# A gated mix of a spectral layer and a SwiGLU on one core: comparisons placed in the second product stage, another VectorE order in the last stage, 4 KB rows of output, a branch hint

## The chip, the core and the metric

The kernel runs on one core of one Trainium2 chip. Its engines are TensorE (PE, whose weight loads the profile lists as PEld), VectorE (DVE), ScalarE (ACT), GpSimd (POOL) and SyncE (SP, which here only issues DMAs). The metric is the time of one execution on the device, in microseconds; the figure of a version is the median of its runs.

## The reference

With x of 2048 x 512, D = 512 and F = 1376, all in float32:

```python
a = einsum("bsd,ed->bse", x, dft_hid_re)
b = einsum("bsd,ed->bse", x, dft_hid_im)
y = einsum("ts,bse->bte", dft_seq_re, a) - einsum("ts,bse->bte", dft_seq_im, b)
h = silu(x @ w1) * (x @ w3)          # 2048 x 1376
g = sigmoid((x * gate_w).sum(-1, keepdims=True))
out = g * y + (1 - g) * (h @ w2)
```

The four DFT matrices are inputs. They are made of cosines and sines, whose rows and columns repeat with signs; the kernel uses that, but only after it has compared the entries it was given with one another.

## The kernel before

Each float32 product is made of three products in a faster format: an operand is split into a high part (rounded by ACT, `high`, L115) and a low part (the rest, taken by DVE, `low`, L118), and `mm3` (L129) adds high x high, high x low and low x high in one bank of accumulators. `split` is `high` and then `low`. So each operand of PE costs one instruction of ACT and one of DVE, about 1.1 us each for 128 x 1024 values.

The work goes in three stages.

**Gate and up products.** F is cut in 11 chunks of 128 columns, the last with 96; rows of x go in two groups. An item is a chunk and a group, with the products of a fast 2 x 2 scheme. `store_h(n, k, h)` (called from L309 on, on POOL's DMA queue) puts the finished h of an item in memory, in `hs`.

**Products with w2.** 22 steps (`HSTEPS`): 11 chunks for one half of the rows, then 11 for the other. A step is 24 products of 128 x 512 into eight banks `H0` to `H7`. Within step m, ACT and DVE make high and low part of the h of step m+2 (`high_h`, `low_h`, the tiles `ht`, read into `hr`), SP starts to load the h of step m+4 (`load_h`), and w2's parts follow the same way. The last chunk, with 96 rows, is done apart: `load_stacked` reads 64 of its rows and two copies of the other 32 into one tile and four pieces of those 32 into a second, and `stacked` multiplies them so that no product has an operand of 32 rows alone, except eight small ones. At the end of each half, ACT writes (1 - g) h w2 as tiles `nb` of two blocks of 128 rows (L1266); those of the first half go to memory (`nbsp`) and come back later (`load_nb`), those of the second half stay in four buffers of their own, `NBK`.

In the gaps of this stage stands everything that the Fourier part needs. A hand-written planner sets it: a `task` has an engine, a cost in us, a load and a number of 4 KB-wide buffers (list `F4`, taken with `wide`, given back with `free`). `load_ahead(t)` starts loads for tasks in order, as long as buffers are left beyond the reserve `RES` and the paced time `NEXT` allows; `work(engine, t, us)` puts tasks whose load was started at least `LAND` us before into the program, up to `us`. In the loop of the steps, `credit` is the time DVE may spend on tasks: 3.0 us a step in the first half, 3.75 in the second. The tasks are:

- the comparisons: 60 tiles of 128 x 1024 entries of the matrices for sequences (`compare_one` and `compare_two`, `equal`, L555), each against the first tile of its group (`rep`), and some smaller ones. The groups are O1a, O1b, O2 and E2. `accum_out` counts the equal entries in columns of `tail`. The late tiles of E2 (i of 8 and more) are compared as two halves of 128 x 2 x 256 with signs +1 and -1.
- the folding of x: sums and differences of rows that meet the same factors (`make_pair`, `odd_part`, `even_part`, tiles `xm`, `xf`), with `fix_a` and `fix_b`, which put two lone rows in their places.
- `mov`, the parts of the matrix for sequences, and `dt`, those of the matrix for the hidden dimension.
- `lone`, which POOL does once, right ahead of step 0: sums and differences of the four quarters of one row of 1024 and of a few other edge values (L973 to L997).

**The last stage.** PE makes folded sums O1 (two halves), O2 and E2 (two halves) from x and the matrix for sequences, each in a pair of banks (`next_two`, four pairs in turn). For O1, ACT copies one part (`e`, L1336), DVE adds and subtracts the other (`s`, L1337 and L1338), and all are split into `z_O`, `z_E`. DVE puts one late comparison behind the `s` of each half of O1, and `work("D", end + 14.0, 2.5)` puts comparisons ahead of the low part of the second z_E. `verdict` (L565 and L566) then counts the columns of `tail` that hold what they should. After that come ten output units: 12 products each with `dt` (Y), g times the result plus `nb` (`r`, L1391, for two blocks of rows or one; the last unit in two pieces, L1395), and a DMA of `r` to `out` on SP (L1399, L1397), with rows of 2 KB. Behind unit 1, `verdict_end` sums the count over partitions by one small product (`count`, L569, in a pair of banks of its own) and DVE turns it into a flag. Behind unit 4's sums PE, ACT and POOL read the flag, and at the end `tc.If(bad > 0)` (L1412) runs the general way, without any folding, where an entry had not been as expected.

```python
    work_until(end + 16.0, range(n_late))
    verdict()
    ...
        if u == 1:
            verdict_end(next_two("count"))
```

Of the kernel before, what the change touches and what calls it, by code (L numbers as in the profile page):

```python
# [13 lines left out]
P = 128  # L14
S = 2048
D = 512
# [15 lines left out]
def fnet_swiglu_gate_kernel(  # L32
# [106 lines left out]
    NZ = misc.shape[-1] - 32 - 2 * (NS + 8)  # L139
    gs = dram.tile([NTB, 1, 512], F32, tag="gs", name="gs")  # L140
    nbsp = dram.tile([S // P, P, D], F32, tag="nbsp", name="nbsp")
    hs = dram.tile([NC, P, S], F32, tag="hs", name="hs")
    wbsp = dram.tile([NC, P, 2, 4, 256], F32, tag="wbsp", name="wbsp")
# [160 lines left out]

    def store_h(n, k, h):

        c, g = ITEMS[n]
        b = 2 * g + k
        nc.gpsimd.dma_start(hs[c][:, b * TB : (b + 1) * TB], h)  # L309
# [285 lines left out]
    def load_ahead(t):  # L595
        CLOCK[0] = t
        load_pairs(t)
        for i in ORDER[:LIMIT[0]]:
            _, _, _, _, f, need, temps = QUEUE[i]
            if i in LOADED:  # L600
                continue
# [148 lines left out]
    def compare(kind):  # L750
# [4 lines left out]
        LAST[kind] = [task("D", 1.24 if kind == "E2" and i > 7 else 1.16, lambda i=i: compare_one(kind, i), (),  # L755
# [45 lines left out]
    def compare_small():  # L801
        d = task("D", 0.4, differ_small, (), lambda: load_t(72, misc[:, 32:]), 1)
        task("A", 0.7, add_small, (d,))
# [43 lines left out]
    def fix_a():  # L847

        nc.gpsimd.tensor_copy(at_first(XR["O1a"], 1), row_v)
        nc.gpsimd.memset(at_first(XR["w", 0], 1), 0.0)  # L850

    def fix_b():
        w = at_first(XR["w", 1], 0)
        nc.gpsimd.tensor_add(edge[:1, :128], w[:, :128], w[:, 128:])
        nc.gpsimd.tensor_sub(edge[:1, 128:256], w[:, :128], w[:, 128:])
        nc.gpsimd.tensor_copy(w, row_u)
# [105 lines left out]
    def lone():  # L962
# [3 lines left out]
        ROWS.extend(wide(f"row{k}") for k in range(2))  # L966
        r0, r1 = ROWS
        nc.sync.dma_start(r0[:1], edges[:, :1024])
        nc.sync.dma_start(rowm[:1], edges[:, 1024:])
        nc.sync.dma_start(spc, misc[:, :32])  # L970
        a, b = r0[:1, :512], r0[:1, 512:]
        u, v = r1[:1, :512], r1[:1, 512:]
        g.tensor_add(u, a, b)  # L973
        g.tensor_sub(v, a, b)
        g.tensor_add(u[:, :256], u[:, :256], u[:, 256:])
        g.tensor_sub(v[:, :256], v[:, :256], v[:, 256:])
# [5 lines left out]
        s = spc.rearrange("p (w t) -> p w t", w=2)  # L982
# [26 lines left out]
        return u[:, :256], v[:, :256]  # L1009
# [61 lines left out]
    R, LEFT = F - (NC - 1) * P, {}  # L1071
    assert R == 96

    def load_stacked(m, half):
# [3 lines left out]
        h = hs[NC - 1][:, half * 1024 : (half + 1) * 1024]  # L1078
        for to, lo, hi in ((0, 32, 96), (64, 0, 32), (96, 0, 32)):
            nc.sync.dma_start(a[to : to + hi - lo], h[lo:hi])  # L1080
        v = h[:32].rearrange("p (a g n) -> p a g n", a=2, g=4)
        for g in range(4):
            nc.sync.dma_start(b[32 * g : 32 * g + 32, :256].rearrange("p (a n) -> p a n", a=2), v[:, :, g])
# [81 lines left out]
    def stacked(to, j, h, w):  # L1165
# [5 lines left out]
        for k in range(8):  # L1171
            p, at = slice(32 * (k % 4), 32 * (k % 4) + 32), 512 + k // 4 * P
# [25 lines left out]
    F4.extend((f4d, f"f4_{k}") for k in range(20, 24))  # L1198
    NBK = [(f4d, f"f4_{k}") for k in range(24, 28)]
# [8 lines left out]
    spc = edge[:, :32]  # L1208
# [11 lines left out]
    for m, (half, c) in enumerate(HSTEPS):  # L1220
        again = m >= NC
        i = m % NC
        last = i == NC - 1
        if m == NC:
            GAP[0], RES[0] = 1.6, 1
        if i == 0:
            H = [bank(b, f"H{half}_{j}") for j, b in enumerate(HB)]
        h, w = HT[m][1], WT[i]
        for j in range(8):
# [19 lines left out]
            if j == 3:  # L1249
                credit += 5.0 if m + 2 >= len(HSTEPS) else 3.75 if again else 3.0  # L1250
# [9 lines left out]
            if last:  # L1260
                k = 8 * half + j
                if j % 2 == 0:
                    nbt = take(NBK if again else F4, [P, 1024], F32, f"nb{k}")
# [3 lines left out]
                if j % 2 and not again:  # L1267
                    nc.gpsimd.dma_start(nbsp[k - 1 : k + 1].rearrange("k p n -> p k n"),
                                        nbt.rearrange("p (k n) -> p k n", k=2))
                    free(NB.pop(k // 2))  # L1270
# [44 lines left out]

    UNITS = [("O1", 512 * v + P * a, 512 * v + 256 + P * a, 2, 0) for a in range(2) for v in range(2)]
# [4 lines left out]
    def load_nb(u):  # L1321
        NB[u] = wide(f"nbr{u}")
        nc.sync.dma_start(NB[u].rearrange("p (k n) -> p k n", k=2),
                          nbsp[2 * u : 2 * u + 2].rearrange("k p n -> p k n"))
# [4 lines left out]
    Z, O1 = {}, {}  # L1329
    for p in range(2):  # L1330
        t = O1[p] = next_two(f"O1_{p}")
# [3 lines left out]
        e, s = wide(f"e{p}"), wide(f"s{p}")  # L1335
# [10 lines left out]
    two = next_two("O2")  # L1346
    for p in range(2):
        ps = two[:, 512 * p : 512 * p + 512]
        forms(ps[:, :256], ps[:, 256:], ("O2",), range(2), p)
    t = parts("z_O2").rearrange("p h a n -> p h (a n)")  # L1350
    split(t[:, 0], t[:, 1], two)
    for p in range(2):
        Z["O2", p] = t[:, :, 512 * p : 512 * p + 512]
    for p in range(2):
# [313 lines left out]
```

## Time and profile before

| | |
|---|---|
| median of three runs | 353.34 us (352.95 to 355.42) |
| the profiled execution, its time | 352.38 us |
| the same, its span in the profile | 350.6 us |
| mean clock granted to TensorE | 0.998 of full speed |
| PE, products of the w2 stage (`H`) | 512 of 380 ns |
| DVE, comparisons of whole and half tiles (L555, `t`) | 54, busy 57.0 us |
| POOL, issues of `hs` from `h` | 34 of 543 ns |
| moved by DMA | 102.13 MB, 291 GB/s in the mean |

The time is that of the whole execution; the span goes from the first to the last record of the profile, 1.78 us less. Busy time is that of instructions in execution. The groups of tiles show who paces whom:

```profile
L129 PE MATMUL H<-w2t,ht 128*128 128x512 f32 x512 | 111.3, 380 | 0.0
...
L555 DVE SCALAR_TENSOR_TENSOR t<-t,rep 128x1024 f32<-128x1024 f32 (+1 forms) x54 | 57.0, 1103 | 0.0
L115 ACT ACTIVATE ht<-hr 128x1024 fp32r<-128x1024 f32 (+1 forms) x20 | 21.0, 1058 | 44.8 <-PE H L129 44.7
L309 POOL DMA_DIRECT2D hs<-h x34 | 18.5, 543 | 121.9 <-DVE h L367 98.3
```

A row gives line, engine, operation, what is written from what with its shape, how often, then busy time and the mean of one in ns, and then the engine's idle time ahead of such instructions and what ended most of it. PE had no idle time ahead of the 512 products with w2, whereas ACT sat idle 44.7 us ahead of the high parts of h, until products of PE were done.

### The profile page before, as it was taken

The page shows a single profiled execution, that of the slowest core. Times are in us where ns is not written, and L with a number is a line of the kernel's source. Part 1 is how long each engine was busy: PE and PEld are TensorE (multiplying, and loading weights), DVE is VectorE, ACT ScalarE, POOL GpSimd, SP SyncE. Part 2 cuts the span into 40 slices and gives each one's busy share as a digit, 9 for nine tenths or more (in the row PEclk, how much of TensorE's full clock was granted, in tenths as well). Part 3 has the DMA queues.
Part 4 walks back from the last instruction along what each step waited for, and adds up shares of the span by engine and source line. Part 5 has one row for each costly group of instructions (what it writes and reads, how often), then busy time and mean ns, then how long its engine had stood idle before and what let it go on. Part 6 is the DMA issues. An engine that isn't in the chain of part 4 may idle for free.

```text
span 350.6 us, 4984 instructions
## 1 busy us (share of the span) xinstructions
PE 343.7 (98%) x1697; PEld 299.3 (85%) x1697; DVE 312.9 (89%) x499; ACT 173.1 (49%) x264; POOL 61.9 (18%) x124
## 2 busy tenths in 40 slices
PE   8999999999999999999999999999999999999993
PEld 4888888888888888888888888888888888889993
DVE  4999989999889988888887799999997998898993
ACT  5875766656546464334442273134679632306400
POOL 0001212112111111111100009981063001000000
PEclk9999999999999999999999999999999999999999
DMA  7638966979559599999999829997156879999066
GB/s 279 259 146 314 351 226 244 371 269 323 215 159 352 219 380 407 417 388 400 407 397 409 325 81 349 396 314 256 65 179 243 296 239 303 367 416 395 10 237 250
DMA packets 32353, 102.13 MB, mean 291 GB/s; under 512 B 5698, under 2 KB 6722, under 8 KB 30276
## 3 DMA queue, kind: packets, MB, share of 16 engines
q1 hardware_dynamic: 27652, 81.84, 64.1%
q0 software_dynamic: 4672, 19.93, 14.6%
q8 instruction: 15, 0.25, 0.3%
q14 instruction: 14, 0.11, 0.1%
HBM read 77.63 MB, written 24.13 MB: 290 GB/s over the span
## 4 chain that ended last, share of the span: by engine, by line
PE 93%; DVE 3%; DMA 1%; ACT 0%; issue 0%; SPq 0%; DVEq 0%
PE H L129 32%; PE X L129 31%; PE Z L129 16%; PE Y L129 11%; PE C L129 3%; DVE t L555 1%; DMA xs_B<-xt 1%; DVE z_O L118 1%; PE O L129 1%; DVE s L1337 0%; DVE z_E L118 0%; DVE s L1338 0%; PE Y_odd L129 0%; ACT e L1336 0%; DVE r L1395 0%
## 5 line engine op out<-in xcount | busy, mean ns | idle before, releaser
L129 PE MATMUL H<-w2t,ht 128*128 128x512 f32 x512 | 111.3, 380 | 0.0
L129 PEld LDWEIGHTS H<-w2t,ht 128*128 128x128 f32 x512 | 96.5, 189 | 14.4 <-issue 0.7
L129 PE MATMUL X<-xo,wb 128*128 128x512 f32 x378 | 88.6, 379 | 0.0
L129 PEld LDWEIGHTS X<-xo,wb 128*128 128x128 f32 x378 | 71.4, 189 | 10.1
L555 DVE SCALAR_TENSOR_TENSOR t<-t,rep 128x1024 f32<-128x1024 f32 (+1 forms) x54 | 57.0, 1103 | 0.0
L115 ACT ACTIVATE ht<-hr 128x1024 fp32r<-128x1024 f32 (+1 forms) x20 | 21.0, 1058 | 44.8 <-PE H L129 44.7
L309 POOL DMA_DIRECT2D hs<-h x34 | 18.5, 543 | 121.9 <-DVE h L367 98.3
L129 PE MATMUL X<-xo,wa 128*128 128x512 f32 x126 | 30.7, 380 | 0.0
L129 PE MATMUL Y<-xo,wa 128*128 128x512 f32 x126 | 30.6, 379 | 0.0
L129 PE MATMUL Z<-xo,wb 128*128 128x512 f32 x126 | 30.6, 379 | 0.0
L129 PE MATMUL Z<-xo,wa 128*128 128x512 f32 x126 | 30.6, 379 | 0.0
L379 ACT ACTIVATE h<-X 128x512 f32<-128x512 f32 x21 | 12.5, 596 | 34.3 <-PE X L129 32.5
L118 DVE TENSOR_TENSOR ht<-hr,ht 128x1024 fp32r<-128x1024 f32 (+1 forms) x18 | 22.0, 1224 | 5.5 <-ACT ht L115 5.4
L129 PEld LDWEIGHTS X<-xo,wa 128*128 128x128 f32 x126 | 23.7, 189 | 3.6 <-ACT h L379 0.3
L129 PEld LDWEIGHTS Y<-xo,wa 128*128 128x128 f32 x126 | 23.8, 189 | 3.4
L129 PEld LDWEIGHTS Z<-xo,wb 128*128 128x128 f32 x126 | 23.8, 189 | 3.4
L129 PEld LDWEIGHTS Z<-xo,wa 128*128 128x128 f32 x126 | 23.8, 189 | 3.4
L115 ACT ACTIVATE wa<-ws 128x768 fp32r<-128x768 f32 (+2 forms) x21 | 16.9, 806 | 11.8 <-PE Z L129 10.6
L118 DVE TENSOR_TENSOR wa<-ws,wa 128x768 fp32r<-128x768 f32 (+1 forms) x22 | 19.3, 879 | 3.8 <-ACT wa L115 3.6
L358 DVE TENSOR_TENSOR u<-u,X 128x512 f32<-128x512 f32 x21 | 14.4, 686 | 7.7 <-PE X L129 7.6
L383 DVE TENSOR_TENSOR h<-h,u 128x512 f32<-128x512 f32 x21 | 14.5, 688 | 5.7 <-ACT h L379 5.7
L266 ACT ACTIVATE s<-X 128x512 f32<-128x512 f32 x21 | 12.5, 596 | 12.0 <-PE X L129 11.7
(219 smaller groups left out, 461.5 us busy)
## 6 DMA issues: line engine op xcount, KB each, us to landing
t<-wt SPq DMA_DIRECT2D x46, 512.0 KB, 10.1
hs<-h POOLq DMA_DIRECT2D x34, 256.0 KB, 6.3
wbsp<-wb POOLq DMA_DIRECT2D x8, 1024.0 KB, 5.3
wb<-wbsp SPq DMA_DIRECT2D x8, 1024.0 KB, 11.6
hr<-hs SPq DMA_DIRECT2D x16, 512.0 KB, 4.5
tt<-wt SPq DMA_DIRECT2D x7, 1024.0 KB, 6.2
ws<-w SPq DMA_DIRECT2D x11, 512.0 KB, 5.0
xs_B<-xt SPq DMA_DIRECT2D x8, 512.0 KB, 4.4
```

The lines of the kernel that those rows point to most:

```text
L115: nc.scalar.activation(hi, src, AF.Copy)
L118: nc.vector.tensor_sub(lo, src, hi.bitcast(F32))
L129: nc.tensor.matmul(ps.rearrange("p (n a) -> p n a", a=2), u, turns(v)[:, some], **kw)
L266: nc.scalar.activation(s1, x, AF.Copy)
L309: nc.gpsimd.dma_start(hs[c][:, b * TB : (b + 1) * TB], h)
L358: nc.vector.tensor_add(u4, u4, x)
L379: nc.scalar.activation(g1, x, AF.Silu)
L383: nc.vector.tensor_mul(g1, g1, u4)
L555: nc.vector.scalar_tensor_tensor(t, t, sign, r, op0=ALU.mult, op1=ALU.is_equal, accum_out=place(n))
```

## The change

Ten things change in the text; the products, and what is compared, stay.

- **Output.** `out` and `nbsp` are laid out as eight blocks of 128 x 1024, so that an output unit of two blocks is stored in rows of 4 KB; the host puts the rows in order.
- **The late E2 tiles** are laid out on the host so that a whole tile of 1024 is compared at once with a repeated quarter of `rep`.
- **The last chunk.** `store_h` writes its 96 rows, a copy of 32 of them, and the pieces (`rest`): three DMAs in place of one. `load_stacked` reads two tiles in place of seven pieces. The eight small products take other rows.
- **`lone`.** The row of 1024 comes as 128 x 4 + 128 x 4 values spread over partitions; the four sums are of 128 x 4 and 128 x 2, and one DMA to memory (`rowsp`) and one back make a row of it, both on POOL's queue.
- **`fix_a` and `fix_b`.** The two copies go from POOL to ACT, the two edge sums from POOL to DVE.
- **Buffers.** The four of `NBK` join `F4`; the second half's `nb` tiles are taken from `F4` too. The first half's `nb` buffers are given back in step 13. `RES` is 6 from step 8 to 10.
- **The planner.** `credit` is 3.15 and 3.9 us a step in place of 3.0 and 3.75, less 1.25 in the very last one; tasks without a load are taken up only when the tasks they wait for have been issued.
- **The last stage's order.** No comparison stands ahead of the low part of the second z_E; that low part moves behind unit 0's sums, and `verdict` ahead of it.
- **The count.** `verdict_end` comes right behind unit 1's products, ahead of its sums, in unit 1's own pair of banks.
- **The branch.** PE gets a hint, `mark_branch_hint_location`, at unit 7's place in the text, that the branch of `tc.If` is likely to be taken.

The core of the diff:

```diff
+        nc.gpsimd.dma_start(to[:R], h[:R])
+        nc.gpsimd.dma_start(to[R:], h[64:R])
+        nc.gpsimd.dma_start(rest[g, 64 * k : 64 * k + 64].rearrange("(q p) n -> p q n", q=2),
+                            h[64:R].rearrange("p (q n) -> p q n", q=2))
...
-            if i in LOADED:
+            if i in LOADED or not f and any(k not in ISSUED for k in after):
...
-            tv, rv = halves(t), halves(r)
-            for h in range(2):
-                equal(tv[:, :, h], rv[:, :, h], 1.0 - 2.0 * h, 512)
+            q = i % 4
+            rv = r[:, 256 * q : 256 * q + 256][:, None].to_broadcast([P, 4, 256])
+            equal(t.rearrange("p (k n) -> p k n", k=4), rv, 1.0 - 2.0 * (q % 2), 1024)
...
-        a, b = r0[:1, :512], r0[:1, 512:]
-        u, v = r1[:1, :512], r1[:1, 512:]
+        a, b = spc[:, 32:36], spc[:, 36:]
+        u, v = rows[:, :4], rows[:, 4:]
         g.tensor_add(u, a, b)
         g.tensor_sub(v, a, b)
...
+        g.dma_start(rowsp.rearrange("k p n -> p k n"), rows.rearrange("p (k n) -> p k n", k=2)[:, :, :2])
+        row = ROWS[0][:1, :512]
+        g.dma_start(row, rowsp.rearrange("k p n -> (k p n)")[None])
...
-        nc.gpsimd.tensor_copy(at_first(XR["O1a"], 1), row_v)
+        nc.scalar.activation(at_first(XR["O1a"], 1), row_v, AF.Copy)
...
-        for to, lo, hi in ((0, 32, 96), (64, 0, 32), (96, 0, 32)):
-            nc.sync.dma_start(a[to : to + hi - lo], h[lo:hi])
...
+        nc.sync.dma_start(a, hs[NC - 1][:, half * 1024 : (half + 1) * 1024])
+        nc.sync.dma_start(b[:, :256], rest[half])
...
-    F4.extend((f4d, f"f4_{k}") for k in range(20, 24))
-    NBK = [(f4d, f"f4_{k}") for k in range(24, 28)]
+    F4.extend((f4d, f"f4_{k}") for k in range(20, 28))
...
-                credit += 5.0 if m + 2 >= len(HSTEPS) else 3.75 if again else 3.0
+                credit += 5.0 if m + 2 >= len(HSTEPS) else 3.9 if again else 3.15
+                if again and c == NC - 1:
+                    credit -= 1.25
...
-        if p:
-            work("D", end + 14.0, 2.5)
-        split(*(z[:, h].rearrange("p (v n) -> p v n", v=2) for h in range(2)),
-              two.rearrange("p (v n) -> p v n", v=2)[:, :, :258])
-    work_until(end + 16.0, range(n_late))
+    low(*put_e2(0))
+    work_until(end + 14.0, range(n_late))
     verdict()
+    last_e2 = put_e2(1)
...
+        if u == 1:
+            verdict_end(ps)
...
+        if n == 2:
+            nc.sync.dma_start(out[u], r)
+        elif not split_up:
+            nc.sync.dma_start(out_of(k), r[:, :D])
         free(r)
-        if u == 1:
-            verdict_end(next_two("count"))
+        if u == 0:
+            low(*last_e2)
+        if u == 7:
+            tc.mark_branch_hint_location("general", "LikelyTaken", engines=(mybir.EngineType.PE,))
...
-    with tc.If(bad > 0):
+    with tc.If(bad > 0, label="general"):
```

`put_o1`, `put_o2` and `put_e2` hold the text that stood in the loops before; `put_e2` does the products and the high part and returns what `low` needs.

On DVE, from the low part of the second half of O1 to the sums of unit 1 (t are compared tiles, rep what they are compared with, tail the counts, r rows of the output), there stood:

```order
L118 TENSOR_TENSOR z_O_2993<-s_2989,z_O_2993 128x1024
L118 TENSOR_TENSOR z_O_3025<-O_2998,z_O_3025 128x1024
L118 TENSOR_TENSOR z_E_3042<-E_0_3028,z_E_3042 128x516
L555 SCALAR_TENSOR_TENSOR t_2862,tail<-t_2862,rep_1964 128x2x256 x2
L118 TENSOR_TENSOR z_E_3061<-E_1_3045,z_E_3061 128x516
L565 TENSOR_SCALAR tail<-tail 128x1
L566 SCALAR_TENSOR_TENSOR tail<-tail 128x80
L1391 SCALAR_TENSOR_TENSOR r_3104<-Y_3091,tail,nb_2867 128x512 x2
L1391 SCALAR_TENSOR_TENSOR r_3121<-Y_3108,tail,nb_2876 128x512 x2
L570 TENSOR_SCALAR tail<-count 1x1
```

and now:

```order
L118 TENSOR_TENSOR z_O_2990<-s_2958,z_O_2990 128x1024
L118 TENSOR_TENSOR z_O_3020<-O_2993,z_O_3020 128x1024
L118 TENSOR_TENSOR z_E_3037<-E_0_3023,z_E_3037 128x516
L577 TENSOR_SCALAR tail<-tail 128x1
L578 SCALAR_TENSOR_TENSOR tail<-tail 128x80
L1419 SCALAR_TENSOR_TENSOR r_3095<-Y_3082,tail,nb_2869 128x512 x2
L118 TENSOR_TENSOR z_E_3080<-E_1_3064,z_E_3080 128x516
L582 TENSOR_SCALAR tail<-Y_3100 1x1
L1419 SCALAR_TENSOR_TENSOR r_3115<-Y_3100,tail,nb_2878 128x512 x2
```

The two half comparisons have left this stretch, the second z_E stands behind unit 0's two sums, the verdict's two instructions ahead of them, and the flag (L570, now L582) is made ahead of unit 1's sums.

On POOL, at the head of `lone`, ahead of step 0 of the w2 products (row is one row of 1024 values, rows its quarters spread over partitions, few some edge values), there stood:

```order
L973 TENSOR_TENSOR row_1894<-row_1893 1x512
L974 TENSOR_TENSOR row_1894<-row_1893 1x512
L975 TENSOR_TENSOR row_1894<-row_1894 1x256
L976 TENSOR_TENSOR row_1894<-row_1894 1x256
L978 TENSOR_TENSOR few<-rowm 1x2
L979 TENSOR_TENSOR few<-rowm 1x2
```

and now:

```order
L983 TENSOR_TENSOR rows<-edge 128x4
L984 TENSOR_TENSOR rows<-edge 128x4
L985 TENSOR_TENSOR rows<-rows 128x2
L986 TENSOR_TENSOR rows<-rows 128x2
L987 DMA rowsp<-rows 128x2x2
L989 DMA row<-rowsp 1x16x32
L991 TENSOR_TENSOR few<-rowm 1x2
L992 TENSOR_TENSOR few<-rowm 1x2
```

The long sums on one partition have become short ones on all, and two DMAs stand behind them.

On ACT, from the leftover of w2 to the first `nb` tiles at the end of the first half (ht are high parts of h, w2t of w2, xf of folded x), there stood:

```order
L115 ACTIVATE left<-w2r_2166 128x512
L1162 ACT_TABLE_LOAD
L1162 ACTIVATE tail<-tail 128x16
L1163 ACTIVATE tail<-tail 128x16
L115 ACTIVATE ht_2279<-hr_2202 128x1024
L115 ACTIVATE w2t_2281<-w2r_2166 128x512
L115 ACTIVATE ht_2319<-hr_2248 128x1024
L115 ACTIVATE xf_O1a<-xm_O1a 128x1024
L115 ACTIVATE ht_2360<-hr_2290 128x1024
L1266 ACTIVATE nb_2362<-H_0_1929,tail 128x512
```

and now:

```order
L115 ACTIVATE left<-w2r_2187 128x512
L784 ACTIVATE size,tail<-dh_2169 128x516
L861 ACTIVATE xo_O1a<-row 1x256
L1170 ACT_TABLE_LOAD
L1170 ACTIVATE tail<-tail 128x16
L1171 ACTIVATE tail<-tail 128x16
L115 ACTIVATE ht_2316<-hr_2231 128x1024
L115 ACTIVATE w2t_2318<-w2r_2187 128x512
L868 ACTIVATE xw_2194<-row 1x256
L115 ACTIVATE ht_2358<-hr_2281 128x1024
L115 ACTIVATE ht_2396<-hr_2327 128x1024
L1282 ACTIVATE nb_2398<-H_0_1940,tail 128x512
```

The two row copies of `fix_a` and `fix_b` (L861, L868) stand here now, the second ahead of the h of step 11, and the high part of folded x has moved behind the `nb` tiles.

More of the change, by code (lines that the diff above doesn't have):

```diff
@@ L1008, in lone @@
         g.tensor_sub(lb[:, 3], sob[:, 0], sob[:, 1])
-        return u[:, :256], v[:, :256]
+        return row[:, :256], row[:, 256:]
     for kind in ("O2", "O1a", "O1b", "E2"):
@@ L1207, in fnet_swiglu_gate_kernel @@
     edge, rowm, few = (own(k, [P, n]) for k, n in (("edge", 258), ("rowm", 520), ("few", 5)))
-    spc = edge[:, :32]
+    spc = edge[:, :40]
+    rows = own("rows", [P, 8])
     two, lone_a, lone_b = own("two", [P, 2, 2, 8]), own("lone_a", [P, 8]), own("lone_b", [P, 4, 2, 2])
@@ L1262, in fnet_swiglu_gate_kernel @@
                 if j % 2 == 0:
-                    nbt = take(NBK if again else F4, [P, 1024], F32, f"nb{k}")
+                    if again:
+                        F4.insert(0, F4.pop(next(i for i, (p, _) in enumerate(F4) if p in (f4d, f4_a))))
+                    nbt = wide(f"nb{k}")
                     NB[k // 2] = nbt
@@ L1322, in load_nb, with put_o1 @@
         NB[u] = wide(f"nbr{u}")
-        nc.sync.dma_start(NB[u].rearrange("p (k n) -> p k n", k=2),
-                          nbsp[2 * u : 2 * u + 2].rearrange("k p n -> p k n"))
+        nc.sync.dma_start(NB[u], nbsp[u])
     for u in range(4, 8):
         load_nb(u)
-    Z, O1 = {}, {}
-    for p in range(2):
-        t = O1[p] = next_two(f"O1_{p}")
+    Z = {}
+    def put_o1(p):
+        t = next_two(f"O1_{p}")
+        e, s = wide(f"e{p}"), wide(f"s{p}")
         for par in range(2):
@@ L1345, in fnet_swiglu_gate_kernel, with put_o2, put_e2 @@
         Z["O1", p] = z
[L1346 to L1354, printed above, removed]
+    def put_o2():
+        two = next_two("O2")
+        for p in range(2):
+            ps = two[:, 512 * p : 512 * p + 512]
+            forms(ps[:, :256], ps[:, 256:], ("O2",), range(2), p)
+        t = parts("z_O2").rearrange("p h a n -> p h (a n)")
+        split(t[:, 0], t[:, 1], two)
+        for p in range(2):
+            Z["O2", p] = t[:, :, 512 * p : 512 * p + 512]
+    def put_e2(p):
         two = next_two(f"E2_{p}")
@@ L1358, in fnet_swiglu_gate_kernel @@
         z = Z["E2", p] = t.rearrange("p (h n) -> p h n", h=2)
-        if p:
-            work("D", end + 14.0, 2.5)
-        split(*(z[:, h].rearrange("p (v n) -> p v n", v=2) for h in range(2)),
-              two.rearrange("p (v n) -> p v n", v=2)[:, :, :258])
-    work_until(end + 16.0, range(n_late))
+        v = [*(z[:, h].rearrange("p (v n) -> p v n", v=2) for h in range(2)),
+             two.rearrange("p (v n) -> p v n", v=2)[:, :, :258]]
+        high(*v[::2])
+        return v
+    for p in range(2):
+        put_o1(p)
+    put_o2()
+    low(*put_e2(0))
+    work_until(end + 14.0, range(n_late))
     verdict()
+    last_e2 = put_e2(1)
     def d_of(k):
@@ L1526 @@
                         got[i, pp, r, im] = row
-        tiles.append(turns(got).reshape(n, P, 1024))
+        got = turns(got)
+        if kind == "E2":
+            four = got[8:].reshape(2, 4, P, 4, 256).transpose(0, 3, 2, 1, 4)
+            got = np.concatenate([got[:8].reshape(8, P, 1024), four.reshape(8, P, 1024)])
+        tiles.append(got.reshape(n, P, 1024))
     k = np.arange(S // 4 // 2 + 1)
@@ L1638 @@
         "xw": xw.reshape(8, P, 2 * D),
-        "misc": np.concatenate([spc.reshape(P, 32), small], 1),
-        "edges": np.concatenate([row.ravel(), turns(ew), turns(dx), sp4])[None],
+        "misc": np.concatenate([spc.reshape(P, 32), row.reshape(4, P, 2).swapaxes(0, 1).reshape(P, 8), small], 1),
+        "edges": np.concatenate([turns(ew), turns(dx), sp4])[None],
         "xt": np.stack(xq, 1).reshape(2, 4, P, 2 * TB),
```

78 lines of the change are left out of this document (39 added, 39 removed).

## The prediction, as it was put on record

> **What bounds the kernel now.** I read the page first (span, busy time, chain), then the busy time by stage, then the end of the chain in order of time, and last the outputs and the program's exit.
>
> ```profile
> span 350.6 us, 4984 instructions
> PE 343.7 (98%) x1697; PEld 299.3 (85%) x1697; DVE 312.9 (89%) x499; ACT 173.1 (49%) x264; POOL 61.9 (18%) x124
> ...
> PE 93%; DVE 3%; DMA 1%; ACT 0%; issue 0%; SPq 0%; DVEq 0%
> ```
>
> TensorE (PE) carries 93% of the chain. By stage (start of the products, products with w2, last stage up to its output products, output products, after the last product):
>
> ```profile
> core 0: us, PE busy (x) PEld busy (x) DVE busy (x) ACT busy (x) POOL busy (x), PEclk, DMA share, GB/s
> 5.23:206.94 201.71, 201.69 (x931) 175.38 (x932) 181.89 (x278) 110.61 (x175) 24.01 (x44) 1.00 0.82 310
> 206.94:319.16 112.22, 112.22 (x530) 97.29 (x530) 106.16 (x173) 54.02 (x77) 37.73 (x76) 1.00 0.82 287
> 319.16:330.83 11.67, 11.67 (x107) 11.67 (x106) 10.23 (x23) 5.44 (x8) 0.00 (x0) 1.00 0.48 177
> 330.83:345.11 14.28, 13.94 (x124) 13.56 (x122) 13.42 (x27) 0.60 (x1) 0.00 (x0) 1.00 0.64 235
> 345.11:350.60 5.49, 0.00 (x0) 0.00 (x0) 0.48 (x1) 0.00 (x0) 0.00 (x0) 0.84 0.46 167
> ```
>
> The first two numbers of a row are its length and PE's busy time. From 5.23 to 345.11 PE idles for 0.02 + 0.34 = 0.36 us, at a granted clock of 1.00. The change gives PE the same products, so all that it can win lies in that 0.34, in the 5.49 us behind the last product, and in the 5.23 us at the start, which it leaves alone. The end of the chain:
>
> ```profile
> 331.54 1.22 DVE t L555 x4
> 332.76 0.61 DVE z_E L118
> 333.37 0.13 DVE tail L565
> ...
> 333.59 0.26 DVE tail L566 x2
> 333.85 0.14 issue
> 333.99 0.19 PE count L569 x2
> 334.18 10.25 PE Y L129 x90
> 344.42 0.68 PE Y_odd L129 x6
> ...
> 345.13 0.48 DVE r L1395
> ```
>
> VectorE (DVE) does two half comparisons at 331.54, the last z_E, then the verdict; `count` on PE waits for the verdict, and 90 products queue behind `count`. That wait is nearly all of the 0.34 us.
>
> **The last stage, step by step.** The late comparison pairs leave: one whole comparison stands there in place of three pairs of halves, and the last z_E moves behind unit 0's sums, so that the verdict no longer waits for either.
>
> ```profile
> 323.11 0.68 DVE L1338 TENSOR_TENSOR s<-e,O 128x512 f32<-128x512 f32 x1
> ...
> 327.49 1.06 ACT L115 ACTIVATE z_O<-s 128x1024 fp32r<-128x1024 f32 x1 [1.89 <-DVE s L1338]
> ...
> 330.83 2.84 PE L129 MATMUL Y<-dt,z_O 128*128 128x258 f32 x24
> ...
> 333.76 2.72 DVE L1391 SCALAR_TENSOR_TENSOR r<-Y,tail,nb 128x512 f32<-128x512 f32 x4
> ```
>
> By these durations DVE ends unit O1's second s at 327.3 (323.8, one comparison of 1.15, z_O 1.13, two s of 0.60), waits for ScalarE's (ACT) high part until 328.4, ends two z_O at 330.7 and the first z_E at 331.3, and the verdict (0.13 + 0.26 and two gaps) at 331.8. Units 0 and 1 occupy PE to 333.67 (24 products, 2.84), so `count` finds the verdict done 1.9 us earlier: **minus 0.34 us**. The small product itself (0.19) stays, now in unit 1's own bank, on no new buffer. Next in line is z_E's second half: unit 0's products end at 332.25, its sums (half of 2.72 for two units) at 333.6, z_E at 334.2; unit 3, first to need its bank, starts near 335.1. Cover 0.9 us; cost nothing.
>
> **The outputs.** Rows grow from 2 to 4 KB for units 0 to 5, and the first sums start 1.5 us earlier (332.3 against 333.76). How the outputs queue:
>
> ```profile
> L1399 SPq DMA_DIRECT2D out<-r x1: 377/377/377, 335.2 to 335.2; - x1
> ...
> DMA to landing us min/median/max: 2.8/2.8/2.8
> ```
>
> ```profile
> L1397 SPq DMA_DIRECT2D out<-r x2: 599/784/968, 345.1 to 345.8; - x2
> ...
> DMA to landing us min/median/max: 3.5/3.7/3.9
> ```
>
> ```profile
> edge<-misc SPq DMA_DIRECT2D x1, 16.0 KB, 1.8
> ...
> 300.00:320.00 20.00, 20.00 (x103) 17.11 (x103) 19.39 (x40) 8.00 (x12) 0.00 (x0) 1.00 1.01 400
> 342.00:346.00 4.00, 3.09 (x28) 2.90 (x26) 2.84 (x5) 0.00 (x0) 0.00 (x0) 1.00 1.03 384
> ```
>
> The first output (512 KB, nothing ahead) lands in 2.8 us; the last pieces, 128 KB each, take 3.5 to 3.9, and the engines are full (share 1.03) with 2 KB rows at 384 GB/s, where 4 KB rows run at 400. A 512 KB unit takes 1.37 us at 384 and 1.31 at 400, so units 0 to 5 save 6 x 0.06 = 0.3 us, and 1.5 more comes from the early start: together more than the 0.7 by which the last landing is over 2.8. I take that 0.7: **minus 0.7 us**. Bounds: 0, if the last pieces wait for something else, and 1.7, down to the 1.8 us of a lone 16 KB load in the list of issues (edge from misc); 2.8 is the nearer row, since it is an output.
>
> **The exit.**
>
> ```profile
> L1412 PEldq COMPARE_BRANCH  x1: 4919/4919/4919, 342.9 to 342.9; - x1
> ...
> L1661 SPq DRAIN  x3: 7/7/7, 349.7 to 350.0; - x3
> ...
> L1661 PEldq DRAIN  x2: 8/8/8, 348.1 to 350.1; - x2
> ```
>
> PE's branch takes 4.92 us and ends at 347.8; SyncE (SP), which waits for the outputs, drains at 349.7. The branch hint can shorten only the former: nothing, as long as the landing gains less than 1.6. The order of instructions shows the hint as PE's first instruction, not by unit 7. What it costs there no row shows: at best nothing, hidden behind the first operands (PE's products begin at 5.23), at worst a fetch of the branch's size that PE waits for in mid-kernel, 4.92 less the 2.2 us of products queued when this branch was issued (342.9 to 345.11): 2.7. I take 0, since warm-up fills the start. The Trainium skill, "Runtime: NRT & Kernel Launch", section "Instruction fetch mechanics", says that an engine keeps only two windows of instructions, fetches in sequence, and stalls for a taken branch outside them: the 4.92 agrees. By that rule a hint armed at the start would be spent or in the way long before the branch, and the sum would be 355.0 in place of 352.3.
>
> **The w2 products (206.94 to 319.16).** PE is full there and stays so if each h arrives in time.
>
> ```profile
> ACT ht L115 <- PE H L129: 47.9, 16, 4.1
> ...
> DVE ht L118 <- ACT ht L115: 5.4, 5, 2.1
> ```
>
> ```profile
> 228.81 1.18 POOL L997 TENSOR_TENSOR lone_b<-two 128x4 f32<-128x4 f32 x1
> ```
>
> ```profile
> 211.59 1.81 POOL L973 TENSOR_TENSOR row<-row 1x512 f32<-1x512 f32 x1
> 213.38 2.24 POOL L974 TENSOR_TENSOR row<-row 1x512 f32<-1x512 f32 x1
> ...
> DMA to landing us min/median/max: 2.6/6.3/10.0
> ```
>
> ```profile
> 214.43 2.28 DVE L555 SCALAR_TENSOR_TENSOR t<-t,rep 128x1024 f32<-128x1024 f32 x1
> ...
> 222.88 1.23 DVE L118 TENSOR_TENSOR ht<-hr,ht 128x1024 fp32r<-128x1024 f32 x1
> ```
>
> A step is 24 products, 5.18 us; h for step m+2 is made in step m, and ACT waits 47.9 us for PE here, so the slack is PE's, not theirs. The tightest h before is step 4's (222.88 + 1.23, then 0.6 for its w2), needed at 206.94 + 4 x 5.18 = 227.7: 3.0 us of slack. It was late because comparisons took 2.28 instead of 1.15 while GpSimd (POOL) added its 512-wide rows. Those adds become four of 128x4 (1.18 in the `lone_b` row) plus two small DMAs: DVE gets about 3 us back in the first steps. In exchange POOL waits for its round trip through memory (stores of h landed in 2.6 to 10.0 us), and `lone_a`, which before ends as `lone_b` starts, comes at 228.8 - 7.4 (all four adds, 211.59 to 219.0) + 4.7 + 1.1 + 10 = 237.2 at worst, where DVE now wants it near 234; h of step 7 (1.1, w2 0.6, and `lone_raw` 0.6) would end at 239.5, needed at 243.2. Cost nothing. ACT gets two short row copies; the second waits for DVE's edge sums near 256, and h of step 11 behind it ends near 258.5 against 262.8. Cost nothing, cover 4 us. E2's late comparisons become eight whole ones in place of sixteen halves (2 x 0.61 against 1.15): 0.6 us of DVE time, off the path. The w2 leftovers load in two DMAs in place of seven, twice, and the last chunk's stores grow by eight POOL issues near 115 to 136 us, whose buffers are wanted two items (18 us) later: nothing. The eight small products only change rows. Second-half `nb` tiles now wait for comparisons, the latest of which DVE ends near 312.6, with ACT wanting them at 316: nothing.
>
> **The sum.** 352.38 (the profiled execution; 350.6 of span and 1.78 around it) - 0.34 - 0.7 = 351.3. The median of the runs shown is 0.96 higher, so the time forecast is 353.34 - 1.04 = 352.3.
>
> **Rivals.** (1) The early outputs change nothing at the end, because the last pieces' 3.5 to 3.9 us are their own: only 0.34 comes, 353.0. For it: they are issued 0.7 us apart and their issue took up to 968 ns; against: the full engines until 346. (2) Slower: the hint at the program's start makes PE wait once for instructions, 352.3 + 2.7 = 355.0; from two such waits (357.7) it is over 1% slower. For it: its place and the 4.92; against: PE's 343.7 busy us show no fetch on the path. (3) Slower: in the w2 stage DVE waits for POOL's round trip or a comparison's tile and an h comes late; it decides from some 3.7 us beyond the worst case above, and each us more is a us of PE: about 354.5. (4) The hint and the early landing both bite, with 1.7 in place of 0.7: 351.3.
>
> **Numbers.** Forecast 0.55, (1) 0.24, (2) 0.07, (3) 0.04, (4) 0.10. The range holds the forecast, (1) and (4): 350.4 is 352.38 - 0.34 - 1.7, and 354.0 is rival 1 with 1.0 for the spread of the three runs (352.95 to 355.42). About 1%, 3.5 us, is what a measurement of this kernel can tell from no change; faster than that needs more than both bounds together (2.04): 0.02. Slower by it needs rival 2 twice or rival 3 badly: 0.03. Within 1%: 0.95.
>
> **What would show it.** Right: no idle of PE before `count`, DVE's verdict before 332.3, the first output issued near 333.8, the last landing near 2.8, PE still full in both large stages. Wrong: a wait of PE's weight loads on h or w2, a gap of 2 to 5 us of PE without a releaser (the hint), last landings still 3.5 or more, or SP's drain behind PE's.

## The result

The changed kernel takes 351.08 us (median of six runs, 350.92 to 351.44), the kernel before 353.58 us (six runs, 352.95 to 355.42): a ratio of 0.992, with a 95% interval of 0.9895 to 0.9945. That is 2.5 us less by the medians, between 1.9 and 3.7 by the interval. The profiled execution of the changed kernel took 351.16 us (span 349.3), 1.22 us less than that of the kernel before (352.38). So half of what the medians gained does not show when the two profiles are compared. In the experiments below, two runs (483 and 1296 us) were disturbed and are left out of all medians and ranges.

The busy time by stage, with the columns of the prediction (start, products with w2, sums of the last stage, output products, after the last product), for the changed kernel:

```profile
5.77:207.15 201.38, 201.38 (x931) 175.64 (x932) 181.80 (x278) 110.50 (x175) 28.02 (x52) 1.00 0.83 313
207.15:319.37 112.22, 112.22 (x530) 97.29 (x530) 103.67 (x169) 55.08 (x79) 29.10 (x73) 1.00 0.83 300
319.37:331.04 11.67, 11.67 (x106) 11.67 (x106) 9.91 (x15) 5.45 (x8) 0.00 (x0) 1.00 0.01 1
331.04:344.92 13.88, 13.88 (x124) 13.53 (x122) 12.30 (x23) 0.60 (x1) 0.00 (x0) 1.00 0.67 264
344.92:349.30 4.38, 0.00 (x0) 0.00 (x0) 0.48 (x1) 0.00 (x0) 0.00 (x0) 1.00 0.38 135
```

The w2 stage is as long as before (112.22 us) and PE is full in it. The output products take 13.88 us in place of 14.28, and the end behind the last product 4.38 in place of 5.49. The end of the chain in order of time:

```profile
328.08 3.13 PE E L129 x28
331.20 2.68 PE Y L129 x24
333.88 0.12 PE Y L581 x2
334.00 10.25 PE Y L129 x90
```

No VectorE work is left in it, and `count` (L581) follows the 24 products without a gap. On VectorE's timeline the verdict is done at about 332.2, 1.6 us ahead of `count`, and the sums then wait for PE:

```profile
331.99 0.24 DVE L578 SCALAR_TENSOR_TENSOR tail<-tail 128x80 f32<-128x80 f32 x1
...
332.58 1.41 DVE L1419 SCALAR_TENSOR_TENSOR r<-Y,tail,nb 128x512 f32<-128x512 f32 x2 [0.34 <-PE Y L129]
```

The outputs (units of 4 KB rows, last pieces), PE's branch and the drains:

```profile
L1427 SPq DMA_DIRECT2D out<-r x6: 332/335/488, 334.0 to 341.3; - x6
...
DMA to landing us min/median/max: 3.7/3.8/3.9
```

```profile
L1425 SPq DMA_DIRECT2D out<-r x2: 391/772/1154, 344.8 to 346.1; - x2
...
DMA to landing us min/median/max: 2.3/2.8/3.2
```

```profile
L1443 PEldq COMPARE_BRANCH  x1: 402/402/402, 342.8 to 342.8; - x1
...
L1696 SPq DRAIN  x3: 7/7/7, 348.5 to 348.8; - x3
...
L1696 PEldq DRAIN  x2: 8/8/8, 345.1 to 348.9; - x2
```

The first output is issued at 334.0 (before: 335.2), the last lands at 346.1 + 2.3 = 348.4, and SP drains at 348.5, 3.6 us behind the last product (before: 4.6).

### The profile page after: what moved, and what is told of

The parts are those of the page before. It is cut to its first block, busy times and chain, and to the rows that moved or that the text cites. A ratio compares the mean times of both kernels' runs of the same rounds, so it can differ in the third digit from the quotient of the medians.

```text
span 349.3 us, 4957 instructions
## 1 busy us (share of the span) xinstructions
PE 343.5 (98%) x1697; PEld 299.6 (86%) x1697; DVE 308.9 (88%) x485; ACT 174.0 (50%) x266; POOL 57.3 (16%) x129
## 4 chain that ended last, share of the span: by engine, by line
PE 97%; DMA 1%; DVE 0%; ACT 0%; SPq 0%; issue 0%
PE H L129 32%; PE X L129 31%; PE Z L129 16%; PE Y L129 11%; PE C L129 3%; PE O L129 2%; DMA xs_B<-xt 1%; PE E L129 1%; PE Y_odd L129 0%; DVE r L1423 0%; ACT xo L115 0%; SPq L201 0%; PE Y L581 0%
## 5 line engine op out<-in xcount | busy, mean ns | idle before, releaser
L567 DVE SCALAR_TENSOR_TENSOR t<-t,rep 128x1024 f32<-128x1024 f32 x46 | 54.0, 1219 | 0.0
L316 POOL DMA_DIRECT2D hs<-h x30 | 16.3, 543 | 108.8 <-DVE h L379 85.6
```

Source lines behind the costliest of these rows:

```text
L316: nc.gpsimd.dma_start(to, h)
L567: nc.vector.scalar_tensor_tensor(t, t, sign, r, op0=ALU.mult, op1=ALU.is_equal, accum_out=place(n))
```

## The experiments

They ran in four groups, each with the kernel before on the same chip; that kernel had medians of 353.62 (17 runs), 353.73 (27), 353.38 (23) and 353.54 us (17) there, and its runs lay between 352.26 and 355.79. A ratio is that to the kernel before of the same group, with its 95% interval. The changed kernel itself ran in the first group alone, so later comparisons with it (351.08 and 351.48 us) reach across groups.

**First group: the hint and the rows.** The changed kernel once more:

> The changed kernel itself, beside the others of this group and the kernel before. Both theories: about 2.3 us under the kernel before (351.1 against 353.5). Its profile is a second look at the end: PE's branch near 0.4 us, the last landing near 348.4.

It took 351.48 us (351.09 to 351.71), ratio 0.9933 (0.9916 to 0.995). SP drained 4.0 us behind the last product. The gain stands, and it is about 2 us.

The changed kernel without the hint:

```diff
-        if u == 7:
-            tc.mark_branch_hint_location("general", "LikelyTaken", engines=(mybir.EngineType.PE,))
```

> The changed kernel without the branch hint. Theory 1 (the prediction): the hint costs and gains nothing, since the last outputs land after PE's branch has ended; the time is that of the changed kernel within 0.3 us, and the profile shows a branch of about 4.9 us that ends near 347.7, under 1 us ahead of SP's drain. Theory 2: in most executions the branch's fetch takes longer than in the one profiled before, and PE's end is what the end waits for; then the time is 1.0 to 2.5 us more than the changed kernel's, with a wider spread, and the runs whose span is long have it behind PE's last product.

The kernel before with the hint alone, the same two lines added, and the label of the branch:

> The kernel before with the branch hint alone. Theory 1: no change (353.5, within 0.3 us), with the spread it had. Theory 2: 1.0 to 2.5 us faster than the kernel before, and the spread of its runs shrinks from 2.5 us to under 1. Both: PE's branch falls from 4.9 to about 0.4 us in the profile, and PE's first product of the warm-up starts about 0.15 us later.

Without the hint the changed kernel took 351.05 us (350.99 to 351.67), with it 351.48: the medians are 0.4 us apart, a little more than theory 1 allows, but the ranges overlap almost wholly. The kernel before with the hint took 353.60 (352.52 to 354.70), ratio 1.0006 (0.9991 to 1.0022), with its full spread. Theory 2, which had the hint gain 1.0 us or more, falls. The branch itself does what the hint says, in the changed kernel without the hint and in the kernel before with it:

```profile
L1441 PEldq COMPARE_BRANCH  x1: 4578/4578/4578, 342.9 to 342.9; - x1
```

```profile
L1414 PEldq COMPARE_BRANCH  x1: 397/397/397, 343.7 to 343.7; - x1
...
L1663 SPq DRAIN  x3: 7/7/7, 350.5 to 350.8; - x3
```

4.6 us become 0.4, but either branch ends ahead of SP's drain, which waits for the outputs (347.5 against 348.9 without the hint, 344.1 against 350.5 with it). The hint stands at 0.8 us of the program and works 342 us later; in the changed kernel it is the row

```profile
L1696 PEldq BRANCH_PREFETCH_HINT  x1: 50/50/50, 0.8 to 0.8; - x1
```

What it costs at the start is small: in the kernel before PE's warm-up begins at 1.57 us without it and at 1.74 with it, and the products with w2 begin within 0.1 us of each other. The Trainium skill, "Runtime: NRT & Kernel Launch", "Instruction fetch mechanics", says that a taken branch outside the two windows held stalls for a fetch; the 4.6 without a hint agree. What the prediction drew from that rule, that an early hint would be spent or in the way, the trace does not bear out.

This profile of the kernel before with the hint held the next clue: PE waited 1.0 us for `count`, not 0.34 (the row gives who waited for whom, the total, how often, the longest):

```profile
PE count L569 <- DVE tail L566: 1.0, 1, 1.0
```

The changed kernel with rows of 2 KB in the output:

```diff
-        if n == 2:
-            nc.sync.dma_start(out[u], r)
-        elif not split_up:
-            nc.sync.dma_start(out_of(k), r[:, :D])
+        if not split_up:
+            nc.sync.dma_start(out[FIRST[u] : FIRST[u] + n].rearrange("k p n -> p k n"),
+                              r.rearrange("p (k n) -> p k n", k=2)[:, :n])
```

> The changed kernel with the output's old layout, rows of 2 KB (512 KB in 256 rows instead of 128). Theory 1: the last landing, which gained about 1 us, loses half of it: 0.3 to 0.5 us more than the changed kernel, and the middle outputs land in 4.0 to 4.5 instead of 3.8 us. Rival: the last pieces' landing hangs on their own two issues on SP (1.6 us together) and not on the queue ahead; then within 0.15 us of the changed kernel.

351.71 us (five runs, 351.19 to 352.01) against 351.48 (351.09 to 351.71). The medians are 0.2 us apart, less than theory 1 says and more than its rival, and the ranges overlap. What theory 1 names as its cause did not show: the outputs landed in 3.9 us in the median against 4.0 with the 4 KB rows, and SP drained 4.0 us behind the last product in both. Whether the rows are worth 0.2 us or nothing is not settled.

**Second group: rows, order and the last issue.** The kernel before with the 4 KB rows alone (the same edit the other way):

> The kernel before with the output's new layout alone (rows of 4 KB). Theory 1: the rows shorten the queue ahead of the last pieces; by the 0.33 us that the changed kernel lost with rows of 2 KB: 0.3 us faster than the kernel before. Rival: the queue ahead empties anyway in the last microseconds, or the rows matter only when the outputs start early: within 0.1 us.

353.99 us (352.25 to 355.79), ratio 1.0015 (0.999 to 1.0039): no gain. (The 0.33 us that the expectation starts from is 0.2 by the medians above.) Its profile shows a wait of 1.4 us for `count`, and where it begins. On SP's and ScalarE's timelines, then in the list of waits:

```profile
291.83 2.93 SPq L1083 DMA_DIRECT2D hr20b<-hs  x4
...
300.68 0.38 SPq L1069 DMA_DIRECT2D hr<-hs  x1
...
299.90 2.01 ACT L115 ACTIVATE ht<-hr 128x1024 fp32r<-128x1024 f32 x2 [3.60 <-PE H L129]
...
307.83 1.06 ACT L115 ACTIVATE ht<-hr 128x1024 fp32r<-128x1024 f32 x1 [5.62 <-DMA hr<-hs]
```

```profile
SPq L1083 <- DMA t<-wt: 1.4, 1, 1.4
...
PE count L569 <- DVE tail L566: 1.4, 1, 1.4
```

In the profile of the kernel before, the same places read:

```profile
291.35 1.73 SPq L1083 DMA_DIRECT2D hr20b<-hs  x4
...
297.53 0.38 SPq L1069 DMA_DIRECT2D hr<-hs  x1
...
299.42 2.01 ACT L115 ACTIVATE ht<-hr 128x1024 fp32r<-128x1024 f32 x2 [3.60 <-PE H L129]
...
304.60 1.06 ACT L115 ACTIVATE ht<-hr 128x1024 fp32r<-128x1024 f32 x1 [2.87 <-PE H L129]
...
322.50 0.69 DVE L1337 TENSOR_TENSOR s<-e,O 128x512 f32<-128x512 f32 x1 [1.44 <-ACT e L1336]
```

The h of the last step was issued 3.15 us later, and its high part came 3.23 us later; 0.48 of both is the whole program's shift (the high part ahead of it, which waits for PE, stands at 299.90 against 299.42). Behind that h VectorE has 15 comparisons and the last stage, with 1.44 us of idle time between, ahead of `s`. So 3.23 - 0.48 - 1.44 = 1.3 us should reach the verdict. In the chain of the kernel with the 4 KB rows its second instruction stands at

```profile
335.30 0.26 DVE tail L566 x2
```

against 333.59 before: 335.30 - 333.59 - 0.48 = 1.23 us, as it should.

The last stage's new order alone, in the kernel before (its three late pairs stay):

```diff
-        if p:
-            work("D", end + 14.0, 2.5)
...
-    work_until(end + 16.0, range(n_late))
+    low(*put_e2(0))
+    work_until(end + 14.0, range(n_late))
     verdict()
+    last_e2 = put_e2(1)
...
+        if u == 1:
+            verdict_end(ps)
...
+        if u == 0:
+            low(*last_e2)
```

> The kernel before with the last stage's new order alone (verdict ahead of the second z_E, that low part behind unit 0's sums, the count in unit 1's own bank ahead of its sums); its three late pairs of half comparisons stay. Theory 3: in the kernel before the verdict comes late by a wait that differs from run to run (0.34 us in the profile of before, 1.0 in that of the kernel with the hint alone), since VectorE is full from 296 us to the verdict and passes on what a late load of h costs it; the order puts the verdict 0.6 us earlier, so it takes 0.3 to 0.6 us of a typical 1 us: 353.0 to 353.3, with PE's wait for count at 0.0 to 0.4 in the profile. Rival (the prediction's size): the wait is 0.34, all of it goes, and 0.3 us is all.

353.95 us (352.68 to 355.27), ratio 1.0014 (0.9992 to 1.0035): neither 0.3 nor 0.6 came. PE's waits in its profile, where the last h had its high part at 308.1:

```profile
PE Y L569 <- DVE tail L566: 0.7, 1, 0.7
PE Y L129 <- DVE z_O L118: 0.3, 1, 0.3
PE Y L129 <- DVE tail L570: 0.3, 1, 0.3
```

The verdict's wait is 0.7 us with the last h about as late as in the profile with 1.4, but where VectorE is late, the low part of `z_O` is late too (second row), and unit 3 waits 0.3 us (third row). The four pairs of banks go in turn, so unit 3 takes that of the second half of E2, which VectorE reads for the second z_E until just ahead of the instruction that the profile names, L570. The order moves the wait, it does not make VectorE earlier.

The changed kernel with the last stage's old order (the diff above the other way):

> The changed kernel with the last stage's old order (verdict behind the second z_E, count in a bank of its own behind unit 1's sums); its one late comparison stays one. Theory 3: with the late pairs gone the verdict ends near 333.0, 0.7 us ahead of unit 1's last product, so nothing waits and the time is that of the changed kernel (351.1 to 351.5). Rival: it is the order that brings the gain; then 0.3 to 1.0 us more than the changed kernel and a wait of PE for count in the profile.

350.81 us (350.33 to 351.07), ratio 0.9926 (0.9897 to 0.9954), no wait for `count`. The order is not what gains. Nor do earlier outputs: here the first one was issued at 334.4, against 334.0 in the changed kernel, and SP drained 3.4 us behind the last product, no later than there.

The changed kernel with the very last piece of output on ScalarE's queue:

```diff
-                nc.sync.dma_start(out_of(k)[:, 256 * a : 256 * a + 256], rv[:, i, a])
+                (nc.scalar if a else nc.sync).dma_start(out_of(k)[:, 256 * a : 256 * a + 256], rv[:, i, a])
```

> The changed kernel with the very last piece of output issued on ScalarE's queue instead of behind the first piece's issue on SP's (which took 0.7 to 1.5 us in the profiles and made the last issue wait until 345.6 to 346.4). Theory A: the late issue sets the end; the piece is issued near 345.5 and lands 0.4 us or more earlier: 350.7 to 351.0. Rival B: pieces issued earlier only wait longer in the DMA engines (the last landing came 3.1 us behind the issue at 345.6, but 2.3 behind that at 346.4), so the end stays where it is, within 0.15 us.

351.38 us (351.11 to 351.78). Rival B stands: the piece is issued at 345.6 and no time is gained.

```profile
L1425 SPq DMA_DIRECT2D out<-r x1: 1181/1181/1181, 344.9 to 344.9; - x1
L1425 ACTq DMA_DIRECT2D out<-r x1: 372/372/372, 345.6 to 345.6; - x1
```

**Third group: the loads of the last chunk's h.** In the list of SP's instructions of the kernel before, with the semaphores that each waits for (DMAHW3 and the like count landings of DMAs; PE and DVE stand for work of these engines), the last chunk's seven loads and the load of the last h stand so:

```
L1080 DMA hr_2672<-hs 64x1024 [waits DMAHW3_49,PE_49]
L1080 DMA hr_2672<-hs 32x1024 [waits DMAHW4_49]
L1080 DMA hr_2672<-hs 32x1024 [waits DMAHW5_49]
L1083 DMA hr20b<-hs 32x2x128 [waits DMAHW6_49,DVE_49]
L1083 DMA hr20b<-hs 32x2x128 [waits DMAHW7_49]
L1083 DMA hr20b<-hs 32x2x128 [waits DMAHW0_49]
L1083 DMA hr20b<-hs 32x2x128 [waits DMAHW1_49]
L708 DMA t_2697<-wt 128x1024 [waits DMAHW2_49,DVE_49]
L708 DMA t_2699<-wt 128x1024 [waits DMAHW3_49,DVE_49]
L708 DMA t_2708<-wt 128x1024 [waits DMAHW4_49,DVE_49]
L708 DMA t_2718<-wt 128x1024 [waits DMAHW5_49,DVE_49]
L1069 DMA hr_2725<-hs 128x1024 [waits DMAHW6_49,PE_49]
```

The program's DMAs on SP use eight completion semaphores (DMAHW0 to 7) in turn, and each DMA waits for the landing of the one eight places ahead of it. A piece of 32 x 256 values takes a place like a tile of 128 x 1024, and the four pieces must wait for the landings of three tiles for comparisons and of the h of the step before. From the last chunk's first load on, eleven DMAs stood ahead of that of the last h; in the changed kernel there are five. The four profiles of kernels with the old planner and the seven loads, by how long a piece (L1083) waited for a tile, in us:

| | a piece waited | last h issued | its high part | output products | execution |
|---|---|---|---|---|---|
| kernel before | not at all | 297.53 | 304.60 | 14.3 | 352.38 |
| with the hint | 0.5 | 298.44 | 306.93 | 15.0 | 353.19 |
| with 4 KB rows | 1.4 | 300.68 | 307.83 | 15.5 | 353.68 |
| with the new order | 1.8 | 299.65 | 308.10 | 16.1 | 354.86 |

The longer a piece waited, the later came the high part of the last h and the longer PE took for the output products. The issue alone does not set the high part: the last h took 6.9 to 8.4 us to land in these four. So the two loads alone, in the kernel before (the eight small products take other rows with them, as in the changed kernel):

```diff
+        nc.gpsimd.dma_start(to[:R], h[:R])
+        nc.gpsimd.dma_start(to[R:], h[64:R])
+        nc.gpsimd.dma_start(rest[g, 64 * k : 64 * k + 64].rearrange("(q p) n -> p q n", q=2),
+                            h[64:R].rearrange("p (q n) -> p q n", q=2))
...
-        for to, lo, hi in ((0, 32, 96), (64, 0, 32), (96, 0, 32)):
-            nc.sync.dma_start(a[to : to + hi - lo], h[lo:hi])
...
+        nc.sync.dma_start(a, hs[NC - 1][:, half * 1024 : (half + 1) * 1024])
+        nc.sync.dma_start(b[:, :256], rest[half])
```

> The kernel before with the last chunk's h stored in two tiles and loaded by two DMAs in place of seven (POOL stores three pieces in place of one); every other engine's order is that of the kernel before. Theory 4: the gain lies here. The four small pieces in front hold up SP, which waits for landings of comparison tiles before it can issue the last of them, so that the last step's h is issued at 297.5 to 300.7 instead of near 295.5; its high part comes up to 3 us late, VectorE's 15 comparisons behind it too, and the verdict with them. Then the h is issued near 296, lands before ScalarE wants it at 304.6, PE waits for count 0.0 to 0.4 us, the time is 352.0 to 352.6 (the kernel before's own fastest runs), and the spread falls under 1.2 us. Rival: the DMA engines are full from 300 us on whatever SP issues, and the h lands as late; then 353.7 with a spread of 3 us.

352.14 us (351.86 to 352.62), ratio 0.9958 (0.9941 to 0.9975): 1.24 us less by the medians, between 0.9 and 2.1 by the interval, and a spread of 0.76 in place of 3.2. Its timelines, and PE's wait:

```profile
291.53 0.33 SPq L1089 DMA_DIRECT2D hr20b<-rest  x1
...
294.58 0.50 SPq L1080 DMA_DIRECT2D hr<-hs  x1
...
304.78 1.06 ACT L115 ACTIVATE ht<-hr 128x1024 fp32r<-128x1024 f32 x1 [2.87 <-PE H L129]
```

```profile
PE count L580 <- DVE tail L577: 0.3, 1, 0.3
```

The last h is issued at 294.58, its high part waits for PE and not for the load, and what is left is the 0.34 us of the profile of before. There the last h was issued 2.95 us later although no piece waited for a tile: from the first to the end of the last, SP's issues took 1.57 us for the three loads of `hr` and 1.73 for the four pieces, here 0.39 and 0.33. In that profile this cost nothing, because the high part waited for PE as well. How much of the gain is due to fewer issues and how much to fewer waits for landings was not separated.

The changed kernel with the seven loads (the diff the other way):

> The changed kernel with the old seven loads of the last chunk's h (and its one store); every other engine's order is that of the changed kernel. Theory 4: the last step's h is issued 1 to 4 us later than at 295.2 and lands as much later; the changed kernel has about 2 us of slack between that h and the verdict (0.5 ahead of s, 1.2 ahead of z_O, 1.7 between verdict and count), so the time grows by 0.3 to 1.5 us and the spread too. Rival: the slack takes all of it, or the loads cost nothing: within 0.2 us of the changed kernel (351.3).

352.98 us (eleven runs, 351.24 to 356.19), ratio 0.9981 (0.9953 to 1.0008): 1.5 to 1.9 us more than the changed kernel, at the upper end of what was expected or over it. Most of the gain is lost, and the spread, 4.95 us, is larger than that of the kernel before. The profiled execution was the slowest (356.19):

```profile
293.62 4.09 SPq L1085 DMA_DIRECT2D hr20b<-hs  x4
...
303.05 0.38 SPq L1071 DMA_DIRECT2D hr<-hs  x1
...
310.65 1.06 ACT L115 ACTIVATE ht<-hr 128x1024 fp32r<-128x1024 f32 x1 [5.64 <-DMA hr<-hs]
```

```profile
SPq L1085 <- DMA t<-wt: 3.6, 4, 1.0
...
PE Y L129 <- DVE z_O L118: 0.8, 1, 0.8
PE Y L129 <- DVE s L1349: 0.6, 1, 0.6
PE Y L129 <- ACT z_O L115: 0.5, 1, 0.5
```

Each of the four pieces waited for a tile, the last h was issued at 303.05, and PE waited in the last stage. Not all of the 5 us that this execution took beyond the changed kernel's are waits: its output products took 17.6 us in place of 13.9, of which the first and the third row are 1.3, and the clock granted to PE there was 0.90 (changed kernel: 1.00). Theory 4 holds both ways, but an earlier h is not all that the changed kernel has. There the same two rows read

```profile
295.24 0.35 SPq L1082 DMA_DIRECT2D hr<-hs  x1
...
306.13 1.06 ACT L115 ACTIVATE ht<-hr 128x1024 fp32r<-128x1024 f32 x1 [3.18 <-DMA hr<-hs]
```

The h took 10.8 us to land, and its high part came 1.5 us later than in the profile of before (304.60). It cost nothing, since VectorE still sat idle 0.52 us ahead of `s` and 1.18 us ahead of the low part of `z_O`: with fewer late comparisons behind it, VectorE has slack.

The old order in the changed kernel once more, without the hint:

> The changed kernel with the last stage's old order and without the branch hint. It tries again what the old order alone gave beside the changed kernel (350.8 against 351.1 to 351.5): if the old order is better by itself, 350.6 to 351.0; if that was chance, 351.1 to 351.5. Without the hint PE's branch takes about 4.9 us and ends near 347.8, ahead of SP's drain: no change from that.

351.08 us (350.57 to 351.58). So the 350.81 was in part chance; the old order is not slower, and a gain over the changed kernel is not established.

**Fourth group: three parts together.** The kernel before with the two loads, the new order and the 4 KB rows (the diffs above in one):

> The kernel before with three parts of the change: two loads for the last chunk's h, the last stage's order with the count in unit 1's bank, and 4 KB rows of output. Left out are the planner's numbers and buffers, the short rows of lone, the whole E2 tiles and the hint. If these three are all that counts: 352.1 (the two loads alone) less 0.3 for PE's wait for count and 0.3 for the rows, so 351.3 to 351.7, with no wait for count in the profile. Rival: the parts left out carry the last 0.8 us; then 352.0 to 352.3.

352.06 us (351.59 to 352.87), ratio 0.9951 (0.9931 to 0.9971). The rival stands: order and rows add 0.1 us to what the two loads give (352.14, in another group), although nothing waits for `count` any more. In its profile the sums stand without a gap until 343.3, whereas the changed kernel's wait for PE from 341.9 on:

```profile
339.24 4.02 DVE L1412 SCALAR_TENSOR_TENSOR r<-Y,tail,nbr 128x512 f32<-128x512 f32 x6
```

```profile
342.28 0.75 DVE L1419 SCALAR_TENSOR_TENSOR r<-Y,tail,nbr 128x512 f32<-128x512 f32 x1 [0.39 <-PE Y L129]
```

Its first output is issued at 334.73 in place of 334.02, and SP drains at 349.2, 4.1 us behind its last product. The last 0.6 to 1.0 us (352.06 to between 351.08 and 351.48) thus come with the parts left out: the whole E2 tiles, the planner's numbers and buffers, the short rows of `lone` with the copies that moved to ACT (the hint by itself gave nothing). They leave one late comparison in place of three pairs. Which of them counts was not taken apart.

## Why the prediction was right, and where it was not

The time lay in the range (352.3, 350.4 to 354.0; measured 351.08 and 351.48) and in its class (within 1%). But the gain was forecast as 1.04 us and was about 2.1 to 2.5, so more than half of it was not in the sum. That the time still lay in the range is luck: the forecast goes by the median, but the range's lower end by the profiled execution's 352.38. From the median it would be 353.34 - 0.34 - 1.7 = 351.3, above the 351.08. By its steps:

- **PE's wait for `count`, minus 0.34.** The wait is gone. With two loads either half of the step is enough: there is no wait in the changed kernel with the old order, and none with the three late pairs under the new order. The size was that of one lucky execution: other profiles of the old loads show 1.0 and 1.4 us. That such waits spread the kernel before over 3.5 us is borne out by the two loads, which leave 0.76 of it; that its fastest runs (352.26) are like the profiled one (352.38) is likely, but no profile shows one of them.
- **"The w2 leftovers load in two DMAs in place of seven, twice ...: nothing."** This is the step that failed. The prediction gave a reason for the stores alone (their buffers are wanted 18 us later) and none for the loads, which are of h and not of w2; it asked neither how long SP issues them nor whose landing each issue waits for. Alone the two loads are worth 1.24 us, and taken out of the changed kernel they cost 1.5 to 1.9.
- **"The median of the runs shown is 0.96 higher"** was carried over as a constant from one kernel to the other. It was the missing term: the unprofiled runs of the kernel before had a wait that the profiled one hardly had. After the change the profiled execution and the median differ by 0.08.
- **The landing, minus 0.7.** The end behind the last product fell from 4.6 to 3.6 and 4.0 us, 0.6 to 1.0: right in size, but not shown to be right in its cause. The step rested on the 4 KB rows and on the earlier first output. (Its 0.7 is the excess of a landing of 3.5 us over 2.8; SP's drain at 349.7 fits a last landing of 345.8 + 3.9, so by its own argument the term was 1.1.) With rows of 2 KB the changed kernel drained 4.0 us behind, as with 4 KB, and both its versions with the old order, whose first output came about 0.4 us later, drained 3.4 and 3.3 behind. Nor did another part alone bring it: 4.1 to 4.2 us stand in the profiles with the rows alone, with the two loads alone and with three parts together, 5.3 with the order alone. What carries it stays open, and the agreement in size may be luck.
- **The late part of z_E, cost nothing:** right in the changed kernel. In the old kernel with the new order, where VectorE was late, it was not free (0.3 us).
- **The hint, nothing:** right, with the branch's fall from 4.6 to 0.4 us off the path.
- **The w2 stage stays full:** right. POOL waited 7.8 us for its store of the row to land, inside the 2.6 to 10.0 allowed, and PE's 112.22 us did not change.

```profile
POOL row L989 <- DMA rowsp<-rows: 7.8, 1, 7.8
```

Of the rivals, (1), without a gain at the landing, is out by the profiles, (2) by the two runs on the hint, and (3) by the full w2 stage. Rival (4) named a time close to those measured, 351.3 against 351.08 and 351.48, but not for its reason: the hint gave nothing.

## What to carry to other kernels

When the profiled execution is faster than the median of its runs by more than the spread of a quiet kernel, look for a wait that differs between executions, and profile again, before summing. Where DMAs take completion semaphores in turn, as here, count the DMAs between a late load and the one that matters, and not their bytes alone: in this program small pieces took as many places as large tiles, and each waited for a landing eight places back. An engine that is full from a late load to the bound's wait passes on each microsecond beyond its slack; here reordering at the end moved such a wait, and an earlier load, or fewer comparisons behind it, removed it.

## What the runs showed that was not expected

A hint at the very start of PE's program, at 0.8 us, still shortened a branch at 343 us from 4.6 or 4.9 to 0.4 us. One of SP's two last issues of 128 KB took 0.7 to 1.7 us in every profile, where most of those of 512 KB took 0.33 to 0.38; issuing the second on ScalarE's queue (0.37 us, at 345.6) left the time where it was.
